# Routed experts: the rows of x for the residual are gathered a second time instead of being copied from buffer to buffer

## The chip, the cores and the metric

The kernel runs on one core of one Trainium2 chip. The metric is the device time of one execution in microseconds. Before the change, three runs gave a median of 771.17 us (766.74 to 772.54). The execution that was profiled took 766.78 us, of which the span from the first to the last instruction is 764.8 us; 2.0 us lie around it.

## What is computed

Three stages in a row, in float32:

```python
attn_out = _attn_ref(q, k, v)               # 4 x 8 heads, 576 positions, window 128, bias by distance
x = attn_out.transpose(0, 2, 1, 3).reshape(2304, 512)
x = moe(x, w_in, w_out, s, b)               # h = relu(x @ w_in); (s*h*h + b) @ w_out, 512 -> 2048 -> 512
# routed experts, 8 of them, 512 -> 1024 -> 512
do_compute = (x @ w_skip) > 0
e_idx = argmax(xc @ w_gate); gate_w = softmax weight of that expert
h = np.maximum(xc[mask] @ w1[e], 0.0)
y[mask] = gate_w[mask, None] * (h @ w2[e])
out[do_compute] = xc + y                    # rows that are not computed: out = x
```

The change lies in the last stage. The residual is the `xc +` of the last line: the row of x itself is added to the output of its expert.

## The kernel before

Until some 550 us into the span, the kernel works through attention and the dense layer in blocks of 384 tokens. Each block of x is written to a DRAM tensor `x2d` and to `out`, and `route` appends the number and the gate weight of each token to a list of its expert in DRAM (`lst`). The last stage, `moe2`, reads these lists: for each expert e and each tile k of 128 list places it runs one step. In the profiled execution there are 15 tiles.

A step (`step`, L811) is a software pipeline over three tiles. While tile a is brought in (`at`), tile b goes through the first product (`e1`), and tile c through the second product and out (`e2`). So three tiles are alive, and each has its rows of x and its list entries in a buffer of its own age: `xg[0]`, `xg[1]`, `xg[2]` (128 x 512 float32 each) and `lt[0]` to `lt[2]` (number and gate weight, 128 x 2). At the start of a step `shift(1)` and `shift(0)` (L802) move both one age on, by VectorE: `lt` at L803, `xg` at L804. Then `gather` (L755) copies the next list entries to `lt[0]` (L757) and issues, on GpSimd's queue, an indirect DMA that brings 128 rows of `x2d` to `xg[0]` (L759). `x_t` (L763) transposes `xg[0]` by TensorE (L765), and ScalarE and VectorE split the result into a rounded part `xth` and a rest `xtl`. `gemm1` (L769) and `gemm2` (L779) are 24 matrix products each; `h_t` (L794) transposes between them. `fin` (L786) computes `og` = product x gate + `xg[2]` by VectorE (L787), copies the list entries to `ls` (L789), and scatters `og` to `out` by an indirect DMA on GpSimd's queue (L790).

So `xg[0]` alone feeds the products. `xg[1]` and `xg[2]` only carry the rows to `fin`, two steps later.

Beside this, a step splits weights of the coming experts: `split` (L624) takes a raw 128 x 1024 piece (512 KB, brought by SyncE's or ScalarE's queue into a ring of 12 places), rounds it by ScalarE (L631) and subtracts by VectorE (L68). An expert has 8 pieces, so steps of experts with a single tile split 8 pieces each; steps of experts with many tiles split few or none. After the last tile, `leave` (L851) runs `step(None, ...)`, one more `shift(1)`, `gemm2` and `fin`.

The order: outside the routed stage a planner orders the instructions by a simulated timeline. From L928 on, `tc.manual_schedule` keeps ScalarE, VectorE and GpSimd in the order of the program; every engine works through its own queue in that order, and waits where a buffer isn't there or isn't free. On GpSimd this order is: gather of a step, scatter of the step, gather of the next step. On VectorE: `shift(1)`, `shift(0)`, L757, pieces of weights and `xtl`, `fin`, the two subtractions of `h_t`. The number of tiles of an expert is only known at run time; every engine takes a branch (L866, L875) after each step.

Of the kernel before, what the change touches and what calls it, by code (L numbers as in the profile page):

```python
# [6 lines left out]
F32 = mybir.dt.float32  # L7
# [10 lines left out]
NT, DM, DFF, NE, FE = 2304, 512, 2048, 8, 1024  # L18
# [15 lines left out]
def body(tc, q_in, k_in, vl, wm, we, wg, wgt, s_in, b_in, mask_in, cst_in, rout_in, ids_in, out):  # L34
# [629 lines left out]
    for j in range(NB):  # L664
        if j:
            split_x(j)
        if j == NB - 1:
            ast.close()
            R = mk("moe2", ast, side="right", reuse_waits="tile")
            ws.free.extend(R.tile([128, 1024], F32, name=f"ring{i}") for i in range(RING))  # L670
            pump()
            later = moe2(tc, locals_ns(locals())).send
# [63 lines left out]
def moe2(tc, L):  # L736
    nc = tc.nc
    main, psum, lst, x2d, out = L.main, L.psum, L.lst, L.x2d, L.out
    cnt, rc, ident, eh, el, split, ws = L.cnt, L.rc, L.ident, L.eh, L.el, L.split, L.ws
    C = L.R  # L740
    xg = [C.tile([128, DM], F32, name=f"xg{i}") for i in range(3)]
    lt = [C.tile([128, 2], U32, name=f"lt{i}") for i in range(3)]
    ls = [C.tile([128, 2], U32, name=f"ls{i}") for i in range(4)]
    la = C.tile([128, NE, NTILE, 2], U32, name="la")
    og = C.tile([128, DM], F32, name="og")
# [9 lines left out]
    def gather(e, k, rows=NT):  # L755
        if (e, k) != (0, 1):
            nc.vector.tensor_copy(lt[0], la[:, e, k, :])  # L757
        idx = la[:, e, k, 0:1] if isinstance(k, int) and (e, k) != (0, 1) else lt[0][:, 0:1]
        nc.gpsimd.indirect_dma_start(  # L759
            out=xg[0], out_offset=None, in_=x2d[0:rows], in_offset=bass.IndirectOffsetOnAxis(ap=idx, axis=0),  # L760
            bounds_check=rows - 1, oob_is_err=False)

    def x_t():  # L763
        for k in range(4):
            nc.tensor.transpose(p_x[:, k * 128:(k + 1) * 128], xg[0][:, k * 128:(k + 1) * 128], ident)  # L765
        nc.scalar.copy(xth, p_x)
        nc.vector.tensor_tensor(out=xtl, in0=p_x, in1=xth.bitcast(F32), op=ALU.subtract)

    def gemm1(p, f, ks=range(4)):  # L769
        n = 3 * ks[0]  # L770
        for k in ks:
            for x, w in ((xth, eh[p, k]), (xtl, eh[p, k]), (xth, el[p, k])):
                nc.tensor.matmul(p_h[f], lhsT=x[:, k * 128:(k + 1) * 128], rhs=w[:, f * 512:(f + 1) * 512],  # L773
                                 start=n == 0, stop=n == 11)
                n += 1
        if n == 12:
            nc.scalar.activation(out=r[:, f * 512:(f + 1) * 512], in_=p_h[f], func=ACTF.Relu)

    def gemm2(p, f):  # L779
        for c in range(4 * f, 4 * f + 4):  # L780
            w, o = 4 + c // 2, (c % 2) * 512
            for i, (h, ww) in enumerate(((hth, eh[p, w]), (hth, el[p, w]), (htl, eh[p, w]))):
                nc.tensor.matmul(p_o, lhsT=h[:, c * 128:(c + 1) * 128], rhs=ww[:, o:o + 512],  # L783
                                 start=c == 0 and i == 0, stop=c == 7 and i == 2)

    def fin(n):  # L786
        nc.vector.scalar_tensor_tensor(out=og, in0=p_o, scalar=lt[2][:, 1:2].bitcast(F32), in1=xg[2],  # L787
                                       op0=ALU.mult, op1=ALU.add)
        nc.vector.tensor_copy(ls[n], lt[2])  # L789
        nc.gpsimd.indirect_dma_start(  # L790
            out=out, out_offset=bass.IndirectOffsetOnAxis(ap=ls[n][:, 0:1], axis=0), in_=og, in_offset=None,
            bounds_check=NT - 1, oob_is_err=False)

    def h_t():  # L794
        for c in range(8):
            nc.tensor.transpose(p_t[c // 4][:, (c % 4) * 128:(c % 4 + 1) * 128], r[:, c * 128:(c + 1) * 128], ident)  # L796
        for f in range(2):
            fs = slice(f * 512, (f + 1) * 512)
            nc.scalar.copy(hth[:, fs], p_t[f])  # L799
            nc.vector.tensor_tensor(out=htl[:, fs], in0=p_t[f], in1=hth[:, fs].bitcast(F32), op=ALU.subtract)  # L800

    def shift(a):  # L802
        nc.vector.tensor_copy(lt[a + 1], lt[a])  # L803
        nc.vector.tensor_copy(xg[a + 1], xg[a])  # L804

    def hint(e, k):

        if e < NE and k < NTILE:
            tc.mark_branch_hint_location(f"tile{e}_{k}", hint=K[e] > k, engines=[mybir.EngineType.PE])

    def step(at, e1, e2, ahead, n=0, wider=0, then=None):  # L811

        pieces = list(range(ws.split, min(ahead, 8 * NE)))
        if e2 is not None:
            shift(1)
        if e1 is not None:
            shift(0)
        if at is not None and at != (0, 1):  # L820
            gather(*at)

        def more(n):
            for _ in range(min(n, len(pieces))):
                split(*divmod(pieces.pop(0), 8))
        if e1 is None:
            x_t()
        more(2)
        if e1 is not None:
            gemm1(e1 % 2, 0)  # L830
            more(2)
            gemm1(e1 % 2, 1)
            for _ in range(min(wider, RING + MORE - ws.places)):
                ws.free.append(extra[ws.places - RING])
                ws.places += 1
            L.pump(nc.scalar)
        if at is not None and e1 is not None and e2 is None:
            x_t()
        more(8)
        if e2 is not None:  # L840
            gemm2(e2 % 2, 0)
            if at is not None:
                x_t()
            if then:
                hint(*then)
            gemm2(e2 % 2, 1)
            fin(n)
        if e1 is not None:
            h_t()

    def leave(e, prev2):  # L851

        if e + 1 < NE:
            step((e + 1, 0), e, prev2, 8 * e + 12, 2 + e % 2, MORE, (e + 1, 1))
        else:
            step(None, e, prev2, 8 * NE, 2)
            shift(1)
            gemm2(e % 2, 0)
            gemm2(e % 2, 1)
            fin(3)  # L860

    def chain(e, k, prev2):

        if k == KMAX[e]:
            st = ws.state()
            with tc.If(K[e] > k, preferred_fallthrough_block=True, label=f"tile{e}_{k}") as c:  # L866
                with tc.For_i(k, K[e], 1) as kk:
                    step((e, bass.ds(kk, 1)), e, e, 0)
                leave(e, e)
            ws.back_to(st)  # L870
            with c.Else():
                leave(e, e)
            return
        st = ws.state()
        with tc.If(K[e] > k, preferred_fallthrough_block=True, label=f"tile{e}_{k}") as c:  # L875
            step((e, k), e, prev2, 8 * e + 12, k % 2, 2 if e == 0 else 0, (e, k + 1))
            chain(e, k + 1, e)
        ws.back_to(st)
        with c.Else():
            leave(e, prev2)  # L880

    nc.gpsimd.memset(xg[0], 0.0)
    nc.vector.tensor_scalar_max(cnt[:, 0:1], cnt[:, 0:1], 128.0)
    nc.sync.dma_start(out=la[:, 0, 0:2], in_=lv[:, 0, 0:2])
    gather(0, 0, NT - TB)
    yield
    p_x = bank("at", "p_x")
    x_t()  # L890
    shift(0)
    shift(1)

    with tc.issue_after((yield)):
        p_h = [bank("ao", "p_h0"), bank("as1", "p_h1")]
# [5 lines left out]
    with tc.issue_after((yield)):  # L901
        p_t = [bank("h", "p_t0"), bank("acc0", "p_t1")]
        p_o = bank("acc1", "p_o")
# [5 lines left out]
    nc.vector.tensor_tensor(out=lt[0][:, 1:2].bitcast(F32), in0=new[:, 1:2], in1=la[:, 0, 1, 1:2].bitcast(F32),  # L909
                            op=ALU.add)  # L910
    gather(0, 1)
    with tc.issue_after(mark):
        gemm2(0, 1)
    yield
    fin(1)


# [3 lines left out]
                            in1=rc[0:1, 32:32 + NTILE].unsqueeze(1).to_broadcast([1, NE, NTILE]), op=ALU.is_gt)  # L921
# [83 lines left out]
```

## Time and profile before

| | |
|---|---|
| median of 3 runs | 771.17 us (766.74 to 772.54) |
| the profiled execution | 766.78 us |
| its span | 764.8 us |
| TensorE busy with matrix products | 731.4 us (96% of the span) |
| VectorE busy | 537.2 us (70%) |
| ScalarE busy | 387.4 us (51%) |
| GpSimd busy | 51.9 us (7%) |
| DMA | 96.39 MB, 126 GB/s on average |

How to read it: busy time is the time in which an engine executes instructions; an engine's idle time just before an instruction is put down to what that instruction waited for. Times at the left of a timeline row are microseconds from the start of the span. PE is TensorE, PEld its loading of weights, DVE is VectorE, ACT is ScalarE, POOL is GpSimd.

### The profile page before, as it was taken

How to read it: one execution, taken by the hardware profiler on the slowest of the kernel's cores; microseconds unless marked ns; L12 is line 12 of the kernel's file. 1: busy time of each engine (PE TensorE's matmuls, PEld its weight loads, DVE VectorE, ACT ScalarE, POOL GpSimd, SP SyncE). 2: the span in 40 equal slices, each digit the busy share in tenths (PEclk: the TensorE clock that was granted, in tenths of full speed). 3: DMA queues.
4: the chain of work that ended last, by engine and by line, in shares of the span. 5: the costliest groups of instructions: out<-in, count | busy, mean ns of one | idle time of the engine just before them, and what ended most of it. 6: DMA issues, size and time to landing. Idle time of an engine off the chain costs nothing.

```text
span 764.8 us, 12722 instructions
## 1 busy us (share of the span) xinstructions
PE 731.4 (96%) x4322; PEld 609.8 (80%) x4322; DVE 537.2 (70%) x1619; ACT 387.4 (51%) x909; POOL 51.9 (7%) x56
## 2 busy tenths in 40 slices
PE   7889999999999999999999999999998999999996
PEld 4568788888878888888888888988786887777884
DVE  5989998667677676777677665799742344999551
ACT  6757686544554445555554432545432243768440
POOL 0000000000001000100001000100221111112111
PEclk9689999999999999999999999999999999999999
DMA  8976432422314122422123111755444342888000
GB/s 243 324 239 190 136 106 66 146 75 72 91 44 133 46 64 67 145 70 73 53 76 108 42 35 36 261 176 169 125 151 130 129 127 86 296 320 333 20 23 16
DMA packets 50592, 96.39 MB, mean 126 GB/s; under 512 B 8554, under 2 KB 25962, under 8 KB 50496
## 3 DMA queue, kind: packets, MB, share of 16 engines
q1 hardware_dynamic: 45600, 85.82, 35.2%
q0 software_dynamic: 2976, 5.59, 2.3%
q10 hardware_dynamic: 1920, 3.80, 1.5%
q8 instruction: 48, 0.79, 0.4%
q14 instruction: 48, 0.39, 0.2%
HBM read 83.83 MB, written 13.65 MB: 127 GB/s over the span
## 4 chain that ended last, share of the span: by engine, by line
PE 80%; issue 7%; DMA 5%; DVE 5%; ACT 1%; SPq 1%; POOL 0%; another core or an unknown queue 0%; POOLq 0%; DVEq 0%; ACTq 0%
PE h_ps L126 27%; PE acc L126 26%; PE p_h L773 7%; PE p_o L783 5%; PE o_ps L126 4%; PE s_ps L126 3%; PE t_ps L126 3%; DMA xg<-x2d,la 2%; DVE wl L68 1%; DMA out<-og,ls 1%; DMA w_words<-wm 1%; PE p_t L796 1%; PE s_ps L124 1%; DMA la<-lst 1%; PE t_ps L124 1%
## 5 line engine op out<-in xcount | busy, mean ns | idle before, releaser
L126 PE MATMUL h_ps<-xh,wh 128*128 128x384 f32 x380 | 132.7, 349 | 0.0
L126 PE MATMUL h_ps<-xl,wh 128*128 128x384 f32 x380 | 128.6, 338 | 0.0
L126 PE MATMUL h_ps<-xh,wl 128*128 128x384 f32 x380 | 128.5, 338 | 0.0
L446 ACT ACTIVATE r<-h_ps 128x384 f32<-128x384 f32 x96 | 47.0, 490 | 112.9 <-PE h_ps L126 94.5
L447 DVE SCALAR_TENSOR_TENSOR r<-r,sb 128x384 f32<-128x384 f32 x96 | 59.0, 614 | 52.6 <-ACT r L446 51.0
L508 DVE CUSTOM_DVE_ANT_0 junk<-x,hp 128x512 bf16<-128x512 f32 x135 | 92.7, 687 | 1.7
L169 ACT ACTIVATE tp<-tp,stat 128x256 f32<-128x256 f32 (+2 forms) x160 | 74.7, 469 | 37.4 <-DVE stat L161 37.1
L126 PE MATMUL acc<-wh,gh 128*128 128x512 f32 x288 | 87.0, 410 | 0.7 <-ACT gh L456 0.7
L126 PE MATMUL acc<-wh,gl 128*128 128x512 f32 x288 | 83.0, 396 | 0.0
L457 DVE SCALAR_TENSOR_TENSOR gl<-r,sb,gh 128x384 fp32r<-128x384 f32 x96 | 59.1, 616 | 33.8 <-ACT gh L456 33.0
L126 PE MATMUL acc<-wl,gh 128*128 128x512 f32 x288 | 82.5, 395 | 0.0
L126 PEld LDWEIGHTS h_ps<-xh,wh 128*128 128x128 f32 x380 | 71.8, 189 | 6.8 <-issue 3.6
L456 ACT ACTIVATE gh<-r,sb 128x384 fp32r<-128x384 f32 x96 | 59.2, 616 | 32.0 <-DVE r L447 30.9
L126 PEld LDWEIGHTS h_ps<-xl,wh 128*128 128x128 f32 x380 | 72.0, 189 | 2.4
L126 PEld LDWEIGHTS h_ps<-xh,wl 128*128 128x128 f32 x380 | 71.9, 189 | 0.0
L161 DVE CUSTOM_DVE_ANT_0 tp<-s_ps,masks 128x256 f32<-128x256 f32 (+2 forms) x160 | 53.1, 377 | 18.4 <-PE s_ps L126 10.6
L126 PEld LDWEIGHTS acc<-wh,gl 128*128 128x128 f32 x288 | 54.1, 189 | 13.2 <-DVE gl L457 0.4
L126 PEld LDWEIGHTS acc<-wl,gh 128*128 128x128 f32 x288 | 54.1, 188 | 12.6
L126 PEld LDWEIGHTS acc<-wh,gh 128*128 128x128 f32 x288 | 49.6, 188 | 10.4 <-issue 3.3
L773 PE MATMUL p_h<-wh,xth 128*128 128x512 f32 x120 | 48.8, 406 | 3.8 <-ACT wh L631 1.7
L605 POOL DMA_INDIRECT lst<-pay,di x18 | 17.8, 987 | 475.7 <-DVE di L603 471.7
L783 PE MATMUL p_o<-wh,hth 128*128 128x512 f32 x120 | 48.6, 405 | 0.4 <-ACT hth L799 0.4
(139 smaller groups left out, 1259.7 us busy)
## 6 DMA issues: line engine op xcount, KB each, us to landing
ring<-we SPq DMA_DIRECT2D x36, 512.0 KB
w_words<-wm SPq DMA_DIRECT2D x30, 512.0 KB
hp<-wgt SPq DMA_DIRECT2D x45, 256.0 KB
more<-we SPq DMA_DIRECT2D x21, 512.0 KB
vt<-vl SPq DMA_DIRECT2D x32, 192.0 KB
x2d<-x SPq DMA_DIRECT2D x17, 256.0 KB
out<-x SPq DMA_DIRECT2D x17, 256.0 KB
more<-we ACTq DMA_DIRECT2D x7, 512.0 KB
```

The source lines that it names most:

```text
L124: return f(*args, **kw)
L126: i = f(*args, **kw)
L161: anchor['v'] = nc.vector.tensor_tensor_reduce(out=t[0:nr, i, c0:c0 + n], in0=ps[i][0:nr, c0:c0 + n], in1=masks[0:nr, 2 * units[u][1] + i, ...
L169: anchor['s'] = nc.scalar.activation(out=t[0:nr, i, c0:c0 + n], in_=t[0:nr, i, c0:c0 + n], func=ACTF.Exp, scale=-1.0, bias=st[0:nr, 0, i:i ...
L446: nc.scalar.activation(out=r, in_=hp, func=ACTF.Relu)
L447: nc.vector.scalar_tensor_tensor(out=r, in0=r, scalar=sb[:, 0:1], in1=r, op0=ALU.mult, op1=ALU.mult)
L456: nc.scalar.activation(out=gh, in_=r, func=ACTF.Identity, bias=sb[:, 1:2])
L457: i = nc.vector.scalar_tensor_tensor(out=gl, in0=r, scalar=sb[:, 1:2], in1=gh.bitcast(F32), op0=ALU.add, op1=ALU.subtract)
L508: nc.vector.tensor_tensor_reduce(out=junk, in0=x2t[j, t], in1=w, scale=1.0, scalar=0.0, op0=ALU.mult, op1=ALU.add, accum_out=lgs[j][:, t, ...
L605: i = nc.gpsimd.indirect_dma_start(out=lst, out_offset=bass.IndirectOffsetOnAxis(ap=di[:, t:t + 1], axis=0), in_=pay[:, t, :], in_offset=N ...
L773: nc.tensor.matmul(p_h[f], lhsT=x[:, k * 128:(k + 1) * 128], rhs=w[:, f * 512:(f + 1) * 512], start=n == 0, stop=n == 11)
L783: nc.tensor.matmul(p_o, lhsT=h[:, c * 128:(c + 1) * 128], rhs=ww[:, o:o + 512], start=c == 0 and i == 0, stop=c == 7 and i == 2)
```

## The change

A tile's rows of x are fetched from `x2d` twice: once to `xg`, for the transposes, and once more to `xf`, by the list entries in `lt[2]`, in the step in which the tile reaches `fin`. `shift` moves only the list entries. Two buffers remain where there were three. The first tile of all is an exception: its rows are copied once, from `xg` to `xf`.

```diff
-    xg = [C.tile([128, DM], F32, name=f"xg{i}") for i in range(3)]
+    xg, xf = C.tile([128, DM], F32, name="xg"), C.tile([128, DM], F32, name="xf")
...
         idx = la[:, e, k, 0:1] if isinstance(k, int) and (e, k) != (0, 1) else lt[0][:, 0:1]
+        fetch(xg, idx, rows)
+
+    def fetch(x, idx, rows=NT):
         nc.gpsimd.indirect_dma_start(
-            out=xg[0], out_offset=None, in_=x2d[0:rows], in_offset=bass.IndirectOffsetOnAxis(ap=idx, axis=0),
+            out=x, out_offset=None, in_=x2d[0:rows], in_offset=bass.IndirectOffsetOnAxis(ap=idx, axis=0),
             bounds_check=rows - 1, oob_is_err=False)
...
-            nc.tensor.transpose(p_x[:, k * 128:(k + 1) * 128], xg[0][:, k * 128:(k + 1) * 128], ident)
+            nc.tensor.transpose(p_x[:, k * 128:(k + 1) * 128], xg[:, k * 128:(k + 1) * 128], ident)
...
-        nc.vector.scalar_tensor_tensor(out=og, in0=p_o, scalar=lt[2][:, 1:2].bitcast(F32), in1=xg[2],
+        nc.vector.scalar_tensor_tensor(out=og, in0=p_o, scalar=lt[2][:, 1:2].bitcast(F32), in1=xf,
                                        op0=ALU.mult, op1=ALU.add)
...
     def shift(a):
         nc.vector.tensor_copy(lt[a + 1], lt[a])
-        nc.vector.tensor_copy(xg[a + 1], xg[a])
...
         if at is not None and at != (0, 1):
             gather(*at)
+        if e2 is not None:
+            fetch(xf, lt[2][:, 0:1])
...
             step(None, e, prev2, 8 * NE, 2)
             shift(1)
+            fetch(xf, lt[2][:, 0:1])
             gemm2(e % 2, 0)
...
-    nc.gpsimd.memset(xg[0], 0.0)
+    nc.gpsimd.memset(xg, 0.0)
...
     x_t()
     shift(0)
     shift(1)
+    nc.vector.tensor_copy(xf, xg)
```

## Rows read from the trace of the kernel before

**Rows 1.** The page, busy time, share of the span and instructions of the engines.

```profile
PE 731.4 (96%) x4322; PEld 609.8 (80%) x4322; DVE 537.2 (70%) x1619; ACT 387.4 (51%) x909; POOL 51.9 (7%) x56
```

**Rows 2.** Windows, 540 to the end: length, busy time (instructions), clock, DMA share, GB/s.

```profile
755.00:764.80 9.80, 2.65 (x12) 1.80 (x10) 0.83 (x2) 0.00 (x0) 0.97 (x1) 0.81 0.01 3
sum 224.80, PE 209.23 PEld 169.45 DVE 125.76 ACT 97.97 POOL 37.82; mean PE 13.95 PEld 11.30 DVE 8.38 ACT 6.53 POOL 2.52
```

**Rows 3.** Waits of PE, 540 to 765: us in total, times, longest.

```profile
PE p_x L765 <- DMA xg<-x2d,la: 3.0, 3, 1.8
PE p_h L773 <- ACT wh L631: 1.7, 1, 1.7
PE p_h L773 <- ACT hth L799: 1.4, 2, 0.7
```

**Rows 4.** Windows, steps: busy PE PEld DVE ACT POOL, clock, DMA share, GB/s.

```profile
642.70:656.00 13.30, 12.57 (x61) 10.11 (x59) 9.42 (x15) 8.68 (x12) 2.34 (x2) 1.00 0.39 126
656.00:669.37 13.37, 12.73 (x61) 10.27 (x60) 12.72 (x19) 10.34 (x14) 2.35 (x2) 1.00 0.91 327
669.37:683.86 14.49, 12.76 (x62) 10.28 (x61) 12.72 (x19) 10.36 (x14) 2.34 (x2) 1.00 0.91 325
683.86:697.29 13.43, 12.88 (x61) 10.13 (x59) 13.31 (x20) 11.02 (x14) 2.34 (x2) 1.00 0.91 322
...
592.46:604.97 12.51, 12.51 (x62) 10.25 (x61) 3.75 (x10) 2.86 (x5) 2.05 (x2) 1.00 0.38 130
```

**Rows 5.** Groups of instructions, shapes apart, 545 to 765: busy, mean ns, idle before.

```profile
L759 POOL DMA_INDIRECT xg<-x2d,la x14 | 16.6, 1184 | 35.1 <-DVE lt L757 16.3 <-PE p_h L773 8.8 <-DMA out<-og,ls 5.6
L790 POOL DMA_INDIRECT out<-og,ls x15 | 15.2, 1015 | 125.0 <-DVE ls L789 124.6 <-DVE og L787 0.4
L804 DVE COPY xg<-xg 128x512 f32<-128x512 f32 x30 | 12.7, 423 | 1.2 <-DMA xg<-x2d,la 1.1
```

**Rows 6.** Timeline, a step with eight pieces of weights: start, us, what.

```profile
689.12 1.02 POOL L790 DMA_INDIRECT out<-og,ls  x1 [10.60 <-DVE ls L789]
...
690.46 0.43 DVE L804 COPY xg<-xg 128x512 f32<-128x512 f32 x1
...
691.68 1.31 POOL L759 DMA_INDIRECT xg<-x2d,la  x1 [1.54 <-PE p_h L773]
...
697.29 0.66 PE L765 MATMUL p_x<-cst,xg 128*128 128x128 f32 x4 [0.56 <-DMA xg<-x2d,la]
...
700.78 0.75 DVE L787 SCALAR_TENSOR_TENSOR og<-p_o,lt,xg 128x512 f32<-128x512 f32 x1
```

**Rows 7.** Timeline of POOL: a gather of a light step, two indirect DMAs back to back.

```profile
540.33 1.00 POOL L605 DMA_INDIRECT lst<-pay,di  x1 [0.30 <-issue]
...
599.91 1.02 POOL L759 DMA_INDIRECT xg<-x2d,la  x1 [1.87 <-DMA out<-og,ls]
```

**Rows 8.** Chains of two stretches, gathers from issue to landing.

```profile
691.68 5.57 DMA xg<-x2d,la
...
578.69 3.36 DMA xg<-x2d,la
```

**Rows 9.** Timeline, the first tile in the dense layer's last products.

```profile
550.52 0.89 DVE L804 COPY xg<-xg 128x512 f32<-128x512 f32 x2 [1.12 <-DMA xg<-x2d,la]
...
552.64 0.96 PE L126 MATMUL acc<-wh,gh 128*128 128x512 f32 x3 [0.68 <-ACT gh L456]
```

**Rows 10.** Line L866, the branches as TensorE's weight queue takes them.

```profile
L866 PEldq COMPARE_BRANCH  x6: 296/330/1437, 631.0 to 753.3; - x6
```

**Rows 11.** Groups of instructions, 640 to 765: subtraction and rounding of weights.

```profile
L68 DVE TENSOR_TENSOR wl<-more,wh 128x1024 fp32r<-128x1024 f32 x28 | 32.6, 1218 | 2.4 <-ACT wh L631 2.3
...
L631 ACT CAST wh<-more 128x1024 fp32r<-128x1024 f32 x28 | 27.7, 1051 | 0.0
```

**Rows 12.** Timeline, the last tile.

```profile
752.71 0.16 DVE L803 COPY lt<-lt 128x2 uint32<-128x2 uint32 x1
...
757.69 0.75 DVE L787 SCALAR_TENSOR_TENSOR og<-p_o,lt,xg 128x512 f32<-128x512 f32 x1 [4.49 <-PE p_o L783]
```

## The prediction

> **What bounds the kernel now.** I read the page first: TensorE is busy 96% of the span, and VectorE, from which the change takes work, 70% [rows 1]. Time can therefore only come out of the few places where TensorE stands idle. So next the windows: from 540 to 755 us, the stretch that the change touches, TensorE is busy 209.23 - 2.65 = 206.58 us of 215.0, idle 8.4 us [rows 2]. That is the most that any relief of another engine could bring here. It is 1.1% of the time, and a good part of it has other causes.
>
> Then the waits of TensorE in that stretch [rows 3]: 3.0 us in three waits for the rows of x, 1.7 us in one and 1.4 us in two at the start of a step, put down to ScalarE. Last the windows from one transpose of x to the next, which is one step [rows 4]. They show two kinds of step. A light one (few weights to split) lasts 12.51 us with TensorE busy for all of it and VectorE for 3.75 us: there VectorE has more than 8 us to spare. In a heavy one (eight pieces of weights) VectorE is busy 12.7 to 13.3 us of 13.4 to 14.5, with 320 GB/s on the DMA engines: there VectorE is nearly full. Four steps are slow in this way, 642.7 to 697.3 us.
>
> **What goes.** 30 copies of 423 ns become one [rows 5]: 29 x 0.423 = 12.3 us of VectorE, two a step, 0.85 us. Between a scatter and the next gather stands a second effect: the gather could not overwrite its buffer before the copy out of it. In the row, that copy ends at 690.46 + 0.43 = 690.89, the gather starts at 691.68, 0.79 us behind it, and 2.56 us behind the start of the scatter [rows 6]. After the change it waits only for the transposes of the step before, long done. Two indirect DMAs back to back lie 0.30 us apart [rows 7], so the gather can start at 689.12 + 1.02 + 0.30 = 690.44, 1.2 us earlier.
>
> What of this reaches the end:
>
> First tile, 550 us. Two copies run from 550.52 to 551.41, and the dense layer's square (L447, from 551.33) is queued behind them on VectorE; TensorE then idles 0.68 us for what follows from it [rows 9]. One copy remains, so 0.43 us goes. Bounds: 0 and -0.68. I take -0.43: each instruction there begins where the one before it ends, from the copy to the idle time.
>
> Of the three waits for rows of x, the first (0.65 us) is that first tile's own landing, and the second (1.80 us, the longest) follows a gather that waits for list entries read from DRAM, not for a copy. Both stay. The third, 0.56 us at 697.29, is the gather of [rows 6]: it starts 1.2 us earlier, so it goes: -0.56.
>
> The remaining idle time of the heavy steps, 1.7 + 1.4 us [rows 3], lies where a step begins, just behind a branch. TensorE's branch at L866 takes from 0.30 to 1.44 us there [rows 10], which is about the size of these waits. The copies don't lie ahead of them. Value 0; bounds 0 and -3.1, if ScalarE's and VectorE's lateness is what TensorE truly waits for.
>
> In the light steps VectorE's 0.85 us was hidden behind TensorE: 0.
>
> **What comes.** 14 further gathers of 256 KB, each 1.02 to 1.31 us of GpSimd [rows 6, 7], some 16 us on an engine that is busy 7% [rows 1]. In its queue a fetch stands behind the gather and ahead of the scatter of the same step. It waits for `lt[2]` and for the previous `fin`, both earlier on VectorE than what the gather needed, so it holds up nothing; behind it only the scatter waits, which comes some 9 us later. What is new is that `fin` waits for the landing. The heavy step of [rows 6]: the fetch starts at 690.44 + 1.31 + 0.30 = 692.05, and `fin` comes at 700.78, which leaves 8.73 us. A landing takes 3.36 us in a quiet stretch and 5.57 us in the heavy one [rows 8]. If the two gathers pass strictly one after the other, the second's rows take another 5.57 - 1.31 = 4.26 us, and it lands at 690.44 + 5.57 + 4.26 = 700.27, 0.5 us ahead of `fin`. So it is hidden, narrowly; this is the tightest of the heavy steps, the other three have 9.3 to 10.4 us by the same working. In light steps the fetch has about as long and lands sooner. Value 0; bounds 0 and, if two gathers together are each twice as slow, the price of the third rival below.
>
> VectorE's work beside it lengthens a gather: it takes 1.31 us where VectorE subtracts weights and 1.02 us in a light step [rows 6, 7]. The longer one is used above. The Trainium skill (SBUF — State Buffer, sections "Who interferes with whom" and "Summary: rules for kernel authors") speaks against a second gather here: a VectorE instruction with two inputs in SBUF and a GpSimd instruction that reads SBUF exclude each other, and the later one blocks until the first is through. The subtraction of weights is of that kind. By that rule gather and fetch would each be held up for as much as one such instruction; the same page adds, as an inference, that this form doesn't stall descriptors. The row shows 0.29 us more and no full block, so the sum goes by the row; what a full block would do here is the fourth rival.
>
> Traffic: 0.26 MB more in a heavy step at 325 GB/s is 0.8 us of DMA time. ScalarE never waits for a piece of weights, idle 0.0 before 28 roundings [rows 11], so pieces arrive ahead of use: 0. If that cover were gone, 0.8 us in each of four steps, 3.2 us.
>
> The end. After the last `shift(1)` one fetch has only two products to hide it. `lt[2]` is there at 752.71 + 0.16 = 752.87 [rows 12]; with the lag of 0.79 us the fetch starts at 753.66, and with the quiet landing of 3.36 us the rows are there at 757.02, 0.67 us before `fin` at 757.69. With 5.57 us it would be 1.5 us late. DMA is quiet there, so 0; bounds 0 and +1.5.
>
> **Sum.** -0.43 - 0.56 = -1.0 us: the profiled execution would go from 766.78 to 765.8 us. The median of the runs stands 4.4 us above that execution, and its own spread is 5.8 us; on the median the forecast is 771.17 - 1.0 = 770.2 us. A measurement of this kernel tells about 1%, 7.7 us, from no change; this is far below it.
>
> **The rivals.**
> 1. The copies were what held up the heavy steps. For it: VectorE busy 13.31 of 13.43 us. Then the four steps go to the 12.51 us of a light one, 0.79 + 0.86 + 1.98 + 0.92 = 4.55 us, and with the first tile 5.0: 766.2 us. Against it: TensorE's idle time there lies mostly behind branches.
> 2. The change doesn't free the gather: GpSimd is held between scatter and gather by something else, for instance the landing of the scatter, to which the trace puts down the wait in a light step [rows 7]. Against it: the fixed 0.79 us behind the copy. Then only the first tile gains: 770.7 us.
> 3. The second gather lands late and `fin` waits: slower. Two gathers share the queue with weights at 325 GB/s; if each then takes twice the 5.57 us, the fetch lands 11.1 us after its start, against 8.7 to 10.4 us (10.2, 9.3, 10.4, 8.7 in the four steps): late by 0.9 + 1.8 + 0.7 + 2.4 = 5.8 us, and VectorE, full in these steps, can't make it up. With the tail's 1.5 us less the first tile's 0.4: +6.9, 778.1 us. It decides from a landing of 8.7 us on; from about 11 us on it costs over 1%. For it: the share of the DMA engines is 0.91. Against it: the row of 5.57 us is itself from such a step.
> 4. Gather and fetch are each held for a whole subtraction, so the fetch lands 2 x (1.22 - 0.29) = 1.9 us later than in the strict order, 8.2 + 1.9 = 10.1 us after its start: late by 0.8 and 1.4 us in two steps, +2.2 - 0.4 = 773.0 us. One subtraction is 1.22 us [rows 11]. Against it: the 1.31 us of the gather of today.
>
> **How the numbers follow.** Forecast 0.53, rivals 0.17, 0.13, 0.11 and 0.06. Except for the upper part of the third, all lie within 1%. The range is that of the cases, widened by the spread of the runs: from 764.5 us (rival 1 in a fast run) to 777.0 us (rival 4 in a slow run, and part of rival 3; what is beyond it is left out). Slower by over 1%: 0.09, the upper part of rival 3 (0.06) and 0.03 for the planner's order, below. Faster by over 1%: 0.04; it would need nearly all the 8.4 us of idle time, or that the planner orders the instructions ahead of the routed stage otherwise, which can go either way. Within 1%: 0.87.
>
> **What would show it.** VectorE's busy time falls by some 12 us to 525, GpSimd's grows by 14 to 18 us, and the gathers number 15 and 14. Heavy steps: the gather 1.3 us behind its scatter's start, no wait of the transposes at the one place, steps still 12.7 to 14.5 us with idle time behind branches; if they fall to 12.5, rival 1. VectorE waiting at `fin` for DMA of `xf` would mean rival 3 or 4; the same at the end alone, the tail's +1.5. Gathers still 2.5 us or more behind the scatter: rival 2. The prediction is wrong if TensorE's idle time from 540 us on changes by more than 5 us either way.

## The result, and the profile after

The changed kernel takes 779.89 us (median of 6 runs, 776.78 to 781.62) against 770.62 us for the kernel before in 6 runs beside it: ratio 1.0119, 95% interval 1.0089 to 1.0148. A later series gave 1.0132 (1.0100 to 1.0164). So it is slower by 9 us, where the prediction said 770.2 us, with 777.0 us as its upper end. Two executions that ran slow as a whole (2311 us of the last experiment's kernel, 3966 us of the kernel before beside it) are left out of the ratios.

The page of the changed kernel, row of the engines, beside [rows 1]:

```profile
PE 734.7 (95%) x4322; PEld 611.7 (79%) x4322; DVE 529.7 (68%) x1590; ACT 387.4 (50%) x909; POOL 68.9 (9%) x70
```

GpSimd has 14 transfers and 17 us more, as forecast. VectorE has 29 instructions less, but only 7.5 us less of busy time, where the prediction had 12.3 us (to 525 us): the copies ran into their neighbours on VectorE. Two copies of `lt`, two of `xg` and the one of L757 filled 0.93 us of the kernel before, ahead of the subtraction of [rows 6]'s step:

```profile
690.88 1.22 DVE L68 TENSOR_TENSOR wl<-ring,wh 128x1024 fp32r<-128x1024 f32 x1
```

They started at 689.95. In the changed kernel the three that remain take 0.49 us (697.36 to 697.85), so a step is relieved of some 0.44 us, not of 0.85. The time of the whole went elsewhere. Windows of the changed kernel from one transpose of x to the next (length, busy PE PEld DVE ACT POOL, clock, DMA share, GB/s), beside [rows 4]:

```profile
605.35:617.85 12.50, 12.50 (x62) 10.24 (x60) 3.22 (x8) 2.86 (x5) 3.05 (x3) 1.00 0.45 148
617.85:633.91 16.06, 12.75 (x62) 10.10 (x60) 7.85 (x12) 6.70 (x9) 3.57 (x3) 0.98 0.50 170
633.91:647.74 13.83, 13.83 (x60) 11.37 (x61) 3.22 (x8) 2.86 (x5) 3.04 (x3) 0.90 0.19 64
647.74:660.82 13.08, 12.75 (x61) 10.27 (x60) 8.92 (x13) 8.69 (x12) 3.15 (x3) 1.00 0.38 118
660.82:675.38 14.56, 12.90 (x62) 10.13 (x60) 12.71 (x18) 10.74 (x14) 3.78 (x3) 1.00 0.93 344
675.38:690.96 15.58, 12.80 (x61) 10.32 (x62) 11.98 (x16) 9.93 (x14) 3.79 (x3) 1.00 0.88 304
690.96:708.14 17.18, 14.29 (x61) 11.45 (x60) 12.28 (x17) 10.31 (x14) 3.94 (x3) 0.90 0.80 278
...
745.81:777.10 31.29, 22.45 (x105) 17.63 (x103) 6.24 (x14) 4.03 (x7) 5.11 (x5) 0.94 0.08 24
```

Three rows of the kernel before, of the same view, that [rows 4] does not have:

```profile
617.47:630.04 12.57, 12.57 (x61) 10.23 (x60) 8.32 (x14) 6.71 (x9) 2.34 (x2) 1.00 0.36 115
630.04:642.54 12.50, 12.50 (x62) 10.24 (x60) 3.74 (x10) 2.86 (x5) 2.05 (x2) 1.00 0.37 132
...
734.91:764.80 29.89, 22.46 (x105) 17.64 (x103) 7.20 (x17) 4.04 (x7) 2.99 (x3) 0.94 0.04 15
```

The two profiled spans differ by 777.1 - 764.8 = 12.3 us, and the windows say where. Step 617.85: 16.06 - 12.57 = 3.5 us. The step behind it, with a clock of 0.90: 13.83 - 12.50 = 1.3 us. The next four: 13.08 + 14.56 + 15.58 + 17.18 against 13.46 + 13.37 + 14.49 + 13.43 as the transposes stand [rows 4], 5.65 us. The end: 1.4 us. Together 11.9 us, and 0.4 us of later start. (This pair differs by more than the medians' 9 us, since the execution of the kernel before that was profiled is a fast one.) The waits of TensorE in the changed kernel, 540 us to the end (us in total, times, longest), beside [rows 3], name the first and the third:

```profile
PE p_x L768 <- DMA xg<-x2d,la: 6.4, 4, 3.3
PE p_h L776 <- ACT wh L631: 5.7, 2, 2.9
PE p_h L776 <- ACT hth L802: 1.7, 2, 1.4
```

The longest wait for rows of x, 3.3 us, ends at 633.91. It is not a wait of `fin`: VectorE never waits for `xf`. GpSimd's timeline in the changed kernel shows what was late there:

```profile
609.89 1.03 POOL L793 DMA_INDIRECT out<-og,ls  x1 [8.84 <-DVE ls L792]
611.25 1.02 POOL L762 DMA_INDIRECT xg<-x2d,la  x1 [0.33 <-issue]
...
622.39 1.03 POOL L793 DMA_INDIRECT out<-og,ls  x1 [8.82 <-DVE ls L792]
627.24 1.54 POOL L762 DMA_INDIRECT xg<-x2d,la  x1 [3.83 <-DVE wl L68]
...
696.23 1.03 POOL L793 DMA_INDIRECT out<-og,ls  x1 [9.84 <-DVE ls L792]
699.19 1.91 POOL L762 DMA_INDIRECT xg<-x2d,la  x1 [1.93 <-PE p_h L776]
```

At 611 us the gather starts 1.36 us behind the start of its scatter, as forecast. At 627 us it starts 4.85 us behind (2.97 before), at 699 us 2.96 (2.56 before, [rows 6]). The releaser in brackets at 627.24 (VectorE's `wl`) is only what ended last by the profile. The chain of the same stretch goes to the scatter:

```profile
597.39 28.95 DMA out<-og,ls x2
626.34 0.02 issue
626.37 0.04 POOLq L762
...
627.24 6.62 DMA xg<-x2d,la
633.86 0.04 issue
633.91 0.48 PE p_x L768
```

The chain runs through the scatter's rows until 626.34. Then come 0.9 us of instructions of GpSimd's queue at L762 (POOLq, the first at 626.37) with the gaps between them, the gather from 627.24 to its landing at 633.86, and the transposes. GpSimd waited until the scatter ahead of it had landed, whose data the gather doesn't need.

### The profile page after: what moved, and what is told of

It reads as the page before. It is cut to its first block, busy times and chain, and to the rows that moved or that the text cites. A ratio compares the mean times of both kernels' runs of the same rounds, so it can differ in the third digit from the quotient of the medians.

```text
span 777.1 us, 12732 instructions
## 1 busy us (share of the span) xinstructions
PE 734.7 (95%) x4322; PEld 611.7 (79%) x4322; DVE 529.7 (68%) x1590; ACT 387.4 (50%) x909; POOL 68.9 (9%) x70
```

## The experiments

Theory 1 below is the bytes of the second gathers, theory 2 GpSimd's queue and its semaphores, theory 3 what was removed.

**No second gather.** The changed kernel with both fetches taken out.

```diff
-        if e2 is not None:
-            fetch(xf, lt[2][:, 0:1])
...
-            fetch(xf, lt[2][:, 0:1])
```

> The changed kernel without its 14 second gathers: fin adds the rows of the first tile throughout, so the residual is left out. The copies stay removed and the gather stays free of them. Theory 1 (the bytes of the second gather delay what else is on the DMA engines) and theory 2 (one more indirect DMA a step costs GpSimd's queue and the bookkeeping of its semaphores at the branches, whatever its size): 769 to 771 us, ratio to before 0.996 to 1.000. Theory 3 (the loss comes with what was removed: gather and weights move against each other): 776 us or more, ratio above 1.006.

Measured: 769.17 us, ratio 0.9966 (0.9938 to 0.9994). The removal of the copies alone gains 0.34%, 2.6 us, so the whole loss comes with the second gather. Theory 3 falls; theories 1 and 2 both said 769 to 771 us. GpSimd's timeline of this kernel, at the place of the long wait:

```profile
622.41 1.02 POOL L793 DMA_INDIRECT out<-og,ls  x1 [10.14 <-DVE ls L792]
624.68 1.89 POOL L762 DMA_INDIRECT xg<-x2d,la  x1 [1.25 <-issue]
```

Here the gather is 2.27 us behind its scatter, not 4.85.

**A narrow second gather.** The same number of transfers, 8 KB each.

```diff
-            fetch(xf, lt[2][:, 0:1])
+            fetch(xf[:, 0:16], lt[2][:, 0:1], cols=16)
```

> The changed kernel with second gathers of 64 bytes a row instead of 2048, 8 KB in all, so fin adds wrong rows in 16 columns and old ones in the rest. All instructions and waits are as in the changed kernel, the traffic isn't. Theory 1: 769 to 771 us, ratio to before 0.996 to 1.001, the waits of TensorE at p_x and at the start of a step back to those of before (3.0 and 3.3 us). Theory 2: 778 to 781 us, ratio 1.010 to 1.014. Theory 3: the same as theory 2.

Measured: 776.49 us, 1.0081 (1.0046 to 1.0117). With a thirty-second of the bytes, more than half of the loss stays, and the gather is again 4.93 us behind its scatter (627.46 against 622.53). The time lies between the forecasts of theory 1 (up to 771 us) and theory 2 (from 778 us on), and its interval overlaps that of the changed kernel. So the transfer costs by being there; what the bytes add isn't told by this run.

**Copies and second gather.** The kernel before, with a second gather to a buffer that nobody reads.

```diff
+        if e2 is not None:
+            fetch(xd[0], lt[2][:, 0:1])
```

> The kernel before, copies and all, with the 14 second gathers on top, to a buffer that nobody reads. Theory 1: the loss of the changed kernel, 778 to 782 us, ratio to before 1.010 to 1.016. Theory 2: the same. Theory 3: 770 to 772 us, ratio 0.998 to 1.003. If fin's wait for the rows were the cause, also 770 to 772, since nothing waits here.

Measured: 777.67 us, 1.0070 (1.0037 to 1.0104), and the gather at 628.94 us is 5.31 us behind its scatter. The time is just under what theories 1 and 2 said, and far from theory 3's 770 to 772 us: the loss needs nothing of what the change removed.

**Adding in DRAM.** No copies and no second gather: `out` already holds x, and the scatter adds to it.

```diff
-        nc.vector.scalar_tensor_tensor(out=og, in0=p_o, scalar=lt[2][:, 1:2].bitcast(F32), in1=xf,
-                                       op0=ALU.mult, op1=ALU.add)
+        nc.vector.tensor_scalar(out=og, in0=p_o, scalar1=lt[2][:, 1:2].bitcast(F32), scalar2=None, op0=ALU.mult)
...
-            bounds_check=NT - 1, oob_is_err=False)
+            bounds_check=NT - 1, oob_is_err=False, compute_op=ALU.add)
```

> Neither copies nor second gathers: out already holds x, and the scatter adds the product to it. The DMA engines then read 256 KB a step more, as with the second gather, but with the scatter and on no instruction of its own. Theory 1: between, 772 to 779 us, since the bytes are there at another time. Theory 2: 769 to 771 us. Theory 3: 776 us or more.

Measured: 771.22 us, 1.0018 (1.0000 to 1.0036). The scatter took 1.58 us of GpSimd in place of 1.02. It is slower than the kernel without a fetch, and gains nothing over the kernel before. The time lies between theory 2's 769 to 771 us and theory 1's 772 to 779, so it decides nothing between them.

**A fourth transfer.** The changed kernel with one more tiny indirect DMA in each step.

```diff
             fetch(xf, lt[2][:, 0:1])
+            fetch(xs[0], lt[2][:, 0:1], cols=16)
```

> The changed kernel with a fourth indirect DMA in each step, of 64 bytes a row (8 KB), into a buffer that nobody reads. Theory 1 (the bytes of the second gather): 8 KB a step is nothing, so 779 to 781 us as for the change. Theory 2 (one more transfer in GpSimd's software queue costs, whatever its size, since its semaphores are evened out at each branch): a fourth transfer costs about as much again as the third, 7 to 9 us: 785 to 790 us, with more time of GpSimd's semaphore instructions at branches and gathers further behind their scatters. If the third transfer only crossed a threshold (the eight semaphores of the queue no longer suffice for a step), the fourth costs less than half of that: 780 to 784 us.

Measured: 778.57 us, 1.0104 (1.0072 to 1.0137): no dearer than three, and under all three forecasts (the lowest 779 to 781 us). Its windows hold the reason: the gather at 624.76 is 2.03 us behind its scatter, and no transpose waits near 631 us. One part of the loss is gone, others have grown: the four heavy steps take 61.3 us (more on them below), and `fin` waits once for `xf`, 1.8 us. So the price is not a price per transfer.

**Plain DMA for the same bytes.** 256 KB a step by SyncE's queue.

```diff
-            fetch(xf, lt[2][:, 0:1])
+            nc.sync.dma_start(out=xf, in_=x2d[nth[0] * 128:nth[0] * 128 + 128])
```

> The changed kernel with the second rows brought by a plain DMA of SyncE (256 KB, 128 rows that lie together in x2d; so the residual is taken from other rows than the token's). Same bytes as the change, in no queue of GpSimd. Theory 1 (bytes): as the change, 777 to 781 us, gathers landing 6 us and more after their issue. Theory 2 (GpSimd's queue and its semaphores): what the narrow gather and the kernel without a fetch leave for the bytes is about 3 us over 769.2, so 770 to 774 us, with the gather at 622 to 628 us about 2.3 us behind its scatter. If SyncE's weight pieces are held up behind this DMA, ScalarE waits for pieces and the time is more than either.

Measured: 770.55 us, 1.0002 (0.9980 to 1.0024). The bytes, brought outside GpSimd's queue, cost 0.36% (2.8 us) over the kernel without a fetch, at most: SyncE's queue, which also brings the weights, may have a part in it. The gather at 626.10 us is 2.28 us behind its scatter.

**No branches.** The numbers of tiles written into the program, in the kernel before and in the changed one.

```diff
-            with tc.If(K[e] > k, preferred_fallthrough_block=True, label=f"tile{e}_{k}") as c:
+            if K[e] > k:
...
-        _, K = nc.values_load_multi_w_load_instructions(ki[0:1, :], min_val=0, max_val=NTILE - 1)
-        K = [k + 1 for k in K]
+        K = [5, 2, 1, 1, 1, 1, 2, 2]
```

> The kernel before with the number of tiles of each expert (5, 2, 1, 1, 1, 1, 2, 2) written into the program, so without reading the counts and without branches in the last stage. Base for the next run. Both theories: TensorE's idle time behind branches goes (1.7 and 1.4 us and some smaller), so 764 to 770 us.

> The changed kernel with the number of tiles of each expert written into the program, so without branches. Theory 2 as bookkeeping at branches: without branches nothing is evened out, and the change costs -2.6 us (copies) + 3 us (bytes), 0 to 2 us over the kernel before without branches. Theory 2 as mere queueing (a third transfer on GpSimd delays the others, branches or not) and theory 1 (bytes): 6 us or more over it, the gathers landing late as in the change.

Measured: 763.35 us (0.9908, 0.9877 to 0.9938) and 765.70 us (0.9939, 0.9915 to 0.9963). Without branches the change costs 765.70 - 763.35 = 2.35 us in place of 9, just over the 0 to 2 us of theory 2 as work at branches, and far from the 6 us of the others. GpSimd's timeline of the changed kernel without branches, in a heavy step:

```profile
699.17 1.03 POOL L793 DMA_INDIRECT out<-og,ls  x1 [9.11 <-DVE ls L792]
700.50 1.02 POOL L762 DMA_INDIRECT xg<-x2d,la  x1 [0.31 <-issue]
701.83 1.93 POOL L762 DMA_INDIRECT xf<-x2d,lt  x1 [0.30 <-issue]
```

Here every gather is 1.33 us behind its scatter, in all steps, as the prediction had it.

**Other semaphores.** What GpSimd does at the branch is in the order of its instructions as built. The software queue has eight semaphores (DMASW0 to 7), given to its transfers in turn. Where the arms of a branch have met again, so that a gather can be reached by several ways, it waits for a whole list of them. The gather of the long wait in the kernel before, the changed one, and the next experiment, each with the semaphore that the scatter just ahead of it signals when it has landed:

```
before:   L759 DMA xg<-x2d,la   waits DMASW4, 2, 5, 0, 6, VectorE, TensorE; scatter ahead: DMASW3
changed:  L762 DMA xg<-x2d,la   waits DMASW5, 4, 6, 2, 7, 1, TensorE; scatter ahead: DMASW6
next:     L762 DMA xg<-x2d,la   waits DMASW5, 6, 2, TensorE; scatter ahead: DMASW1
```

In the changed kernel the list holds the scatter's own semaphore, DMASW6, and in the profile the instruction of GpSimd's queue that waits for it goes at 626.37, right behind the scatter's landing at 626.34. In the second profile of this kernel (below) the scatter lands at 625.57 and the instruction goes at 625.59. In the kernel before the scatter has DMASW3, which isn't in the list. Nor is the scatter's semaphore in the list of the kernel without a fetch (DMASW3) or of the one with a fourth transfer in each step (DMASW1); these gathers were some 2 us behind. It is in the list of the narrow gathers' kernel and of the one with copies and fetch (DMASW6 in both), 4.93 and 5.31 us behind. So it is not the length of the list that decides (five before, six after the change) but whether the scatter's semaphore is in it. The next kernel has a fourth, tiny transfer in three steps only, ahead of that branch, which shifts the turns:

```diff
             fetch(xf, lt[2][:, 0:1])
+            if e2 == 0 and e1 == 0:
+                fetch(xs[0], lt[2][:, 0:1], cols=16)
```

> The changed kernel with one more tiny transfer (64 bytes a row, into a buffer that nobody reads) in the three steps in which expert 0 is in both products, and in no other step. In the order of GpSimd's instructions as built, the gather behind the branch at 622 us no longer waits for the semaphore that the scatter just ahead of it uses; in the changed kernel it does, as the third transfer has moved the semaphores on by one a step. If that wait is a part of the loss (3.3 us of TensorE idle at 633.9 and 1.3 us of low clock behind it), then three transfers more make the kernel faster: 775 to 777 us, no wait of the transposes at 631 to 634 us, gather 2 to 2.5 us behind its scatter. If each transfer costs by its mere number, 780 to 782 us.

Measured: 774.10 us, 1.0049 (1.0029 to 1.0068): with three transfers more, 5.8 us less than the changed kernel (0.7% of ratio, 5.4 us; by the two intervals between some 2.7 and 8.1 us), and a little less than the 775 to 777 us expected. Its windows and its GpSimd timeline:

```profile
618.84:631.41 12.57, 12.57 (x61) 10.24 (x60) 7.93 (x12) 6.71 (x9) 5.06 (x3) 1.00 0.39 125
631.41:643.91 12.50, 12.50 (x62) 10.24 (x61) 3.22 (x8) 2.86 (x5) 3.05 (x3) 1.00 0.48 168
```

```profile
623.38 1.03 POOL L793 DMA_INDIRECT out<-og,ls  x1 [7.73 <-DVE ls L792]
625.41 2.02 POOL L762 DMA_INDIRECT xg<-x2d,la  x1 [1.00 <-DVE lt L757]
```

The step that took 16.06 us takes 12.57, the one behind it 12.50 at full clock, exactly as before the change. So that wait lies in the order of the semaphores, and it is the largest single part of the loss that an experiment took away.

**Copies on ScalarE.** The kernel before, relieved in another way.

```diff
-        nc.vector.tensor_copy(xg[a + 1], xg[a])
+        nc.scalar.copy(xg[a + 1], xg[a])
```

> The kernel before with the two copies of a step on ScalarE in place of VectorE. VectorE is relieved as in the change, with no transfer more. If VectorE's copies cost the 2.6 us that the kernel without the second fetch has gained, 768 to 770 us; ScalarE is busy 10.3 to 11.0 of 13.4 us in heavy steps and takes 0.6 us for such a copy, so 1.2 us more there: if it then becomes the bound, 771 to 774 us.

Measured: 772.44 us, 1.0024 (1.0006 to 1.0042). No gain over the kernel before, and no version here beats it with the residual in it. But two things of opposite sign lie in this time. The four heavy steps take 53.0 us, less than in any other profile with branches. The first tile pays for it: its two copies stand in ScalarE's queue ahead of what TensorE waits for (a row of ScalarE, then one of TensorE).

```profile
550.42 1.27 ACT L804 COPY xg<-xg 128x512 f32<-128x512 f32 x2 [2.67 <-DMA xg<-x2d,la]
```

```profile
553.44 1.65 PE L126 MATMUL acc<-wh,gh 128*128 128x512 f32 x3 [1.57 <-ACT gh L456]
```

TensorE idles 1.57 us there (0.68 before [rows 9]), and the stretch to the next tile's transposes takes 27.2 us at a mean clock of 0.81, against 22.0 us at 1.00 in the kernel before. A version that moves only the later copies to ScalarE was not run.

**Both kernels again.** Second profiles.

> The changed kernel once more, for a second profile. If TensorE's two long branches (5.9 us, at 676 and 692 us) belong to the change, they are there again with the same lengths; if they come and go with the traffic of one execution, their lengths differ by a microsecond or more, while the wait at 633.9 us, which is in the order of the semaphores, is the same.

> The kernel before once more, for a second profile. TensorE's branches in the four steps with eight pieces took 3.4, 3.7, 4.8 and 3.1 us in the first one; the same question as for the changed kernel. No wait of the transposes at 630 us in either.

Measured: 779.03 us in 5 runs (1.0132) for the changed kernel, though the one execution profiled took 772.68 us; 772.28 us for the kernel before. The wait is there again in the changed kernel (2.08 us, gather 4.83 us behind its scatter), and not in the kernel before. The heavy steps are another matter. TensorE's branch behind each (duration ns min/median/max, then start), first the two longest of the changed kernel's first profile, then three of the kernel before in its first, and three in its second:

```profile
L880 PEldq COMPARE_BRANCH  x1: 5864/5864/5864, 676.5 to 676.5; - x1
...
L880 PEldq COMPARE_BRANCH  x1: 5972/5972/5972, 692.0 to 692.0; - x1
```

```profile
L875 PEldq COMPARE_BRANCH  x1: 3710/3710/3710, 657.0 to 657.0; - x1
...
L875 PEldq COMPARE_BRANCH  x1: 4812/4812/4812, 670.4 to 670.4; - x1
...
L875 PEldq COMPARE_BRANCH  x1: 3050/3050/3050, 684.9 to 684.9; - x1
```

```profile
L875 PEldq COMPARE_BRANCH  x1: 5852/5852/5852, 657.3 to 657.3; - x1
...
L875 PEldq COMPARE_BRANCH  x1: 447/447/447, 674.3 to 674.3; - x1
...
L875 PEldq COMPARE_BRANCH  x1: 5326/5326/5326, 687.2 to 687.2; - x1
```

The first branch ends at 676.5 + 5.9 = 682.4, and TensorE's wait of 2.78 us ends at 682.49; the second at 698.0, and the wait of 2.90 us at 698.12. So the waits that the profile puts down to ScalarE (`wh`, `hth`) are these branches. The kernel before had 3.7, 4.8 and 3.1 us at its three places in the first profile, and 5.9, 0.4 and 5.3 in the second. From 656 us three steps took 41.3 us there, and then:

```profile
656.28:673.25 16.97, 14.19 (x62) 11.39 (x61) 12.73 (x19) 10.33 (x14) 2.35 (x2) 0.90 0.82 301
673.25:686.12 12.87, 12.74 (x62) 10.10 (x60) 12.87 (x20) 10.63 (x14) 2.35 (x2) 1.00 0.90 310
686.12:702.70 16.58, 14.34 (x60) 11.45 (x61) 12.42 (x18) 10.03 (x14) 2.35 (x2) 0.90 0.86 310
```

That is 46.4 us, against 47.3 and 44.3 us in the two profiles of the changed kernel. Long branches stand in both kernels and come and go with the execution. So the 5.65 us that the first pair of profiles showed there can't be put down to the change by these rows alone.

**Neither bytes nor that wait.** Narrow second gathers, and the three tiny transfers.

```diff
-            fetch(xf, lt[2][:, 0:1])
+            fetch(xf[:, 0:16], lt[2][:, 0:1], cols=16)
+            if e2 == 0 and e1 == 0:
+                fetch(xs[0], lt[2][:, 0:1], cols=16)
```

> The changed kernel with the second gathers narrow (64 bytes a row, so the residual is left out but for 16 columns of wrong rows) and the three tiny transfers of the kernel before the last two, by which the gather behind the branch at 622 us waits for no scatter. If the loss is made of three parts that add up, this wait (5.4 us, from that kernel against the changed one), the bytes (3 us, from the narrow gathers against the changed kernel) and the rest (GpSimd's longer drain at the end, 1.1 to 1.4 us, and its semaphore instructions), then 779.5 - 5.4 - 3 = 771 us, 770 to 773. If the narrow gathers' 776.5 us had another cause, it stays at 775 us or more.

Measured: 775.80 us, 1.0051 (1.0022 to 1.0080). The 771 us expected are missed: once the wait is gone, no difference shows between full gathers (1.0049, 1.0029 to 1.0068) and narrow ones (1.0051). So a price of the bytes above some 2.7 us is ruled out by the two intervals; a smaller one is not. Nor did the bytes lengthen the long wait: it was 2.00 us with narrow gathers, 3.31 and 2.08 us with full ones. What is left comes with the third transfer whatever its size: 1.0051 - 0.9966 = 0.85%, 6.5 us over the kernel without a fetch.

Of this the end of the program shows a part. GpSimd's instructions at its last line in the kernel before, the changed kernel, and the kernel with four transfers a step:

```profile
L1001 POOLq DRAIN  x3: 45/107/3987, 759.9 to 764.5; - x3
```

```profile
L1007 POOLq INC_SWDGE_SEM  x5: 461/580/689, 610.0 to 697.6; - x5
...
L1007 POOLq DRAIN  x3: 45/107/5131, 771.1 to 776.8; - x3
```

```profile
L1010 POOLq DRAIN  x3: 45/107/6274, 769.1 to 776.0; - x3
```

The last drain lasts 4.0, 5.1 and 6.3 us: 1.14 us more for each transfer that is added to every step (narrow ones too: 5131 ns there). The semaphore instructions (INC_SWDGE_SEM) on the executed way are 8 before and 13 after, half a microsecond to 1.4 us each. The last of them, ahead of the drain, grew from 1.1 to 1.4 us. So the end costs 1.4 us. In the heavy steps the gathers start 3.0 us behind their scatters (1.9 to 2.3 without a fetch) and land 6.1 to 6.5 us later (medians of the two profiles) in place of 5.4 to 5.7. In the last kernel TensorE waits for such a gather at 670.58 (1.79 us) and here, on its timeline:

```profile
704.05 1.12 PE L768 MATMUL p_x<-cst,xg 128*128 128x128 f32 x4 [3.58 <-DMA xg<-x2d,la]
```

The kernel without a fetch has no such wait behind 600 us. The four heavy steps together (from the transposes of the first to those of the next light step) bear this out over all kept profiles with branches. Without a third transfer they take 54.8 and 59.3 us (kernel before), 56.0, 56.1, 57.1 and 53.0 (no fetch, adding in DRAM, plain DMA, copies on ScalarE), a mean of 56.0 us. With it they take 60.4 and 57.2 us (changed kernel), 60.9, 61.0, 58.7, 61.9 and 61.3 (narrow, copies and fetch, three tiny transfers, both, a fourth transfer), a mean of 60.2 us. That is 4.2 us more, one execution each, with ranges that touch. TensorE's waits for the rows of x within them are 0.25 us on average without it and 2.4 us with it. So about half of these 4 us are gathers that come late; what the other half is (TensorE's branches, its clock) stays open.

## Why the prediction was wrong

The step that failed is this one: a fetch "waits for `lt[2]` and for the previous `fin`, both earlier on VectorE than what the gather needed, so it holds up nothing", with its companion for the gather, "After the change it waits only for the transposes of the step before, long done". Both weigh what the data need. A transfer in GpSimd's queue also takes a semaphore, and behind a branch the next gather waits for a list of them; with a third transfer a step that list held the semaphore of the scatter just ahead (DMASW6), so the gather at 627 us stood still until the scatter had landed at 626.34, and TensorE idled 3.3 us. Value taken: 0. Measured: 5.4 us (the kernel with three tiny transfers more against the changed one), about 1.4 us at the end, and some 5 us more that come with the transfer whatever its size, less 2.6 us for the copies: 5.4 + 1.4 + 5 - 2.6 = 9.2 us. The 5 us are what is left of the 6.5 us, so that the sum comes out is no proof of it; the heavy steps' 4.2 us are the evidence for that part.

Point by point:

- Gather 1.2 us earlier: so in light steps whose gather has no list to wait for (1.36 us behind the scatter at 611 us), and everywhere without branches (1.33 us). In the heavy steps, for which the term was made, the arms of a branch meet between scatter and gather, and the gather came 0.4 us later (2.96 us behind, against 2.56). The row of 2.56 us [rows 6] held 0.9 us of semaphore instruction beside the copy's hold; the prediction read all of it as the copy's.
- The 0.56 us at 697.29: gone at that place, but 0.25 us came back at 675.38. Too small to matter.
- First tile, -0.43 us: TensorE's idle time went from 0.68 to 0.49 us, 0.19 us of the 0.43.
- Copies: the prediction's -1.0 us is within the interval of the kernel without a fetch (-0.5 to -4.8 us). Rival 1 (-5.0 us) is just beyond it. The term of VectorE, 12.3 us, was mis-sized (7.5 us), since the mean length of a copy counts what overlaps with its neighbours; nothing hung on it.
- Heavy steps' idle time lies behind branches: right, and more so than the prediction could show. It took the branch for 0.30 to 1.44 us [rows 10], where the branch that ends these steps is another line (L875, 3.1 to 4.8 us).
- Fetch in time for `fin`: right for the changed kernel, where VectorE never waits for `xf` in either profile. With the tiny transfers in addition it does, once: 1.6 us in the kernel with three of them, 1.8 us in the one with a fourth in each step. Rival 3 did not happen, though its 778.1 us is near the measured time; a near number by a mechanism that did not occur is no credit to it. Rival 4's hold did happen (below), but delayed no `fin` here.
- Traffic 0: right as far as the profiles tell; behind 640 us ScalarE waits for no piece of weights in either profile of the changed kernel.
- The end: not +1.5 us by a late landing, as the bound had it, but 1.4 us of drain behind the last scatter.
- Rival 2 named the place, a gather held by "the landing of the scatter", and priced only the gain that would then be lost (770.7 us), since it took the hold for something that is there already. What it lacked was that the change itself could bring it about.
- The prediction's own sign of being wrong, TensorE's idle time from 540 us on changing by more than 5 us, came true in the first pair of profiles: 15.6 us before, 24.6 us after. In the second pair it is 17.5 and 21.4 us.
- Gathers beside subtractions: the prediction read "0.29 us more and no full block" out of one row. That row is a full block for the rest of a subtraction that was already running. The subtraction of 690.88 (shown at the start) ends at 692.10; the gather starts 0.80 us into it, at 691.68, and ends at 692.99, 0.89 us behind that end [rows 6]. In the changed kernel the gather of 699.19 takes 1.91 us and ends at 701.10, again 0.89 us behind the end of the subtraction that was running:

```profile
698.99 1.22 DVE L68 TENSOR_TENSOR wl<-more,wh 128x1024 fp32r<-128x1024 f32 x1
```

Over all kept profiles, 111 gathers and fetches behind 590 us start at least 0.06 us into a subtraction of weights. Every one ends 0.87 to 0.92 us behind the end of that subtraction, and they take 1.03 to 2.03 us. The 146 that start while none is running, or with one (within 0.02 us), take 1.00 to 1.05 us. The Trainium skill (SBUF — State Buffer, "Who interferes with whom" and "Summary: rules for kernel authors") says that a VectorE instruction with two inputs in SBUF and a GpSimd instruction that reads SBUF block each other, the later one until the first is through; these rows agree with it for the gather, and do not bear out the inference that the prediction quotes beside it, that this form doesn't stall descriptors. The other half they do not show: 28 subtractions that start during a transfer of GpSimd of the short kind take 1.22 to 1.23 us, no more than usual.

## What to carry to other kernels

One more transfer in GpSimd's queue is not free where the engine has idle time: count the semaphores it takes, and look behind every branch, in the order of instructions as built, whether the next transfer waits for the semaphore of the one just ahead of it. Where a gather behind a branch starts well after its scatter and the chain of waits runs through that scatter's landing, the semaphore is the suspect, and a tiny transfer that shifts the turns is a cheap test. Compare several executions before a stall of 3 us behind a branch is put down to an edit: it may come and go in both kernels.

## What the runs showed of the hardware that was not expected

TensorE's clock fell to its lower level (0.50, 1.2 GHz) behind the wait of 3.31 us, and was back at 2.4 GHz by 637 us. The windows of the changed kernel (length, busy time, clock, DMA share, GB/s):

```profile
634.00:635.00 1.00, 1.00 (x5) 1.00 (x6) 0.00 (x0) 0.00 (x0) 0.00 (x0) 0.50 0.42 162
637.00:638.00 1.00, 1.00 (x6) 0.78 (x5) 0.00 (x0) 0.00 (x0) 0.00 (x0) 1.00 0.00 0
```

In the second profile the same wait lasted 2.08 us, the clock stayed at 1.00 behind it, and the step that follows took 12.54 us in place of 13.83. So 1.2 us more of waiting were followed by a step that is 1.3 us longer. The length of a wait alone doesn't decide it: in the first profile of the changed kernel the wait of 2.78 us that ends at 682.49 was followed by a clock of 1.00, and the one of 2.90 us that ends at 698.12 by 0.51. A branch of TensorE in the stretch with 300 GB/s and more on the DMA engines took 4.8 us in one execution of the kernel before and 0.4 us at the same place in another; without branches (763.35 us) that kernel is 7 us faster, nearly as much as the whole loss by this change.
